# Relu pieces and rests of k taken off GpSimd, rests of q put on it, in a biased attention with two MLPs

## The chip, the core and the metric

The kernel runs on one NeuronCore of one Trainium2 chip. The metric is the device time of one execution in microseconds (us). In the profile's rows PE is TensorE, PEld its weight loads, DVE VectorE, ACT ScalarE, POOL GpSimd and SP SyncE, which issues nearly all transfers. L208 is line 208 of the kernel before.

## What is computed

The attention has 2 batches, 8 heads, 576 positions and a head size of 64. Each head gets a bias from a small network of the relative position; the result then runs through two MLPs (1152 tokens, width 512).

```python
scores = scale * np.matmul(q, k.transpose(0, 1, 3, 2))
psi_rel = np.log1p(np.abs(rel))
psi_i = np.log1p(np.maximum(pos[:, None].astype(np.float32), 1.0))
x = (psi_rel / psi_i)[..., None]
h = np.maximum(x @ w1 + b1, 0.0)
bias = h @ w2
scores = scores + bias.transpose(2, 0, 1)[None, :, :, :]
attn = np.exp(scores - max); attn = attn / (sum + 1e-09)
...
x = _moe_ref(...)       # (h * clip(h + 3, 0, 6) / 6) @ w_out, h = x @ w_in
x = _moe2_ref(...)      # (x @ w_a * (x @ w_b)) @ w_out
```

## The kernel before

The kernel is written engine by engine in a fixed order: each engine runs its instructions in the order of the code, and waits by semaphores where it needs another's result. It has three stages.

**The bias ahead of the attention (0 to 31.7 us).** The rows of the bias are made in 36 sets of 16 rows (`s`, later `g`). For one set, `bias_relu` makes four relu pieces `ht` of 128 partitions and `Dd` columns (576 for set 0, falling by 16 a set to 304 at set 17, then rising again to 576 at set 35): each is one instruction over the table `ltab`, on VectorE (L208), ScalarE (L210) or GpSimd (L212) by a letter in a string such as `"VVGA"`. `bias_parts` multiplies the four pieces by `w2` on TensorE (L227) and takes the result out of PSUM into a tile `E`, in forward order on ScalarE (L235) and reversed on VectorE (L244; in the attention steps mostly on ScalarE, L242), and then SyncE writes `E` to a scratch in DRAM (L256). The first ten sets (0 to 9) are done here. Sets 0 to 7 make up the first 128 rows of the bias, which SyncE then reads back (`bias_load`, L276). Even sets and the last two use `"VVVA"`, sets 1, 3, 5, 7 use `"VVGA"`; the pieces of GpSimd for these four lie in tiles of their own (`early`) and are issued ahead of the loop. All this has pools of two sets' buffers (`h`, 8 buffers) and four of `E`.

**The attention (31.7 to about 192 us)** in 36 steps `n`, each for 128 query rows and two heads. A step multiplies q by k (L307), where q and k are each split into a rounded part and a rest, so that the precision of f32 is kept: `q_hi`/`k_hi` round (ScalarE L141 and L167, VectorE L171, GpSimd L169), `q_lo`/`k_lo` subtract (L146, L175). `KS` holds the rounded k of two heads in partitions 0 to 63 and the rest in 64 to 127, and every L307 reads all 128 of them: a step needs both parts of its k. Then VectorE adds the bias and takes the minimum of the negated scores, in two instructions of 576 columns (L313, a custom one and a read of the accumulator each), ScalarE takes the exponential (L317, two of them), VectorE adds 1e-9 to the two sums (L321) and takes their reciprocals (L325), GpSimd scales P by them (L330, two instructions), and one step later TensorE transposes P (L340, L350), which VectorE (L341, L354) and ScalarE (L352) copy out of PSUM; another step later comes P times v (L365, L368), taken out by L377 (ScalarE) and L383 (VectorE). Steps 0 to 25 also carry one set of the bias each (sets 10 to 35), whose four pieces were made in the step before, by `"VVGA"`. `q_lo(n + 2)` is issued near the end of step `n`: on VectorE in steps 0 to 25, on GpSimd in the few left.

The order within a step on VectorE is: two L313, two L208, L321, L325, L383, L146, L341, L354, and then what the table `K_PLAN` has for the end of the step. Its entries are a step (-1 is ahead of step 0, 1.5 is within step 2), and what is done: a rounded part (`hi`), a rest (`lo`) or a load of k for the pair of heads `j`, on the engine given. Steps 0 to 7 are the first to use the pairs `j` = 0 to 7.

**The MLPs (192 to 619 us)** are matmuls on TensorE with the work around them on the other engines.

Of the kernel before, what the change touches and what calls it, by code (L numbers as in the profile page):

```python
# [21 lines left out]
NSET = S // 16  # L22
# [13 lines left out]


K_PLAN = {
    -1: (("hi", 2, "A"), ("lo", 2, "V"), ("hi", 3, "A"), ("hi", 4, "A"), ("lo", 3, "G"), ("load", 6, None)),
    1.5: (("lo", 4, "G"),),  # L40
    2: (("hi", 5, "V"),),
    3: (("lo", 5, "G"), ("load", 7, None), ("hi", 6, "A")),
    4: (("lo", 6, "V"),),
    5: (("hi", 7, "V"), ("lo", 7, "G")),
}
U32 = mybir.dt.uint32

# [2 lines left out]
def kernel(ctx, tc, cons, qm, qt, kt, vm, vt, wm, out):  # L50
# [31 lines left out]
    negb = ph.tile([128, 1], F32, name="negb")  # L82
    cst4 = ph.tile([128, 1], F32, name="cst4")
    cst3 = ph.tile([128, 1], F32, name="cst3")
    RELU = "VVGA"


    idle = ph.tile([128, S], F32, tag="h", bufs=8, name="idle")
# [84 lines left out]
    def k_lo(j, eng):  # L173
        hi, lo = (KS[64 * i : 64 * i + 64, 2 * j : 2 * j + 2, :] for i in range(2))
        eng.tensor_tensor(out=lo, in0=kr[j], in1=hi.bitcast(F32), op=ALU.subtract)  # L175
# [13 lines left out]
    extra = {}
    for i in range(2):  # L190
        t = pb.tile([128, 9, 128], F32, tag="PT", bufs=2, name="early").rearrange("p a n -> p (a n)")
        extra[1 + 4 * i], extra[3 + 4 * i] = t[:, 0:S], t[:, S : 2 * S]

    def bias_relu(s, kinds=RELU, only=None):

        i0, R, Dd = bias_geom(s)
        if s not in h_tiles:
            h_tiles[s] = [ph.tile([128, S], F32, tag="h", bufs=8, name="ht") for _ in range(4 if s not in extra else 3)]
            if s in extra:
                h_tiles[s].insert(kinds.index("G"), extra[s])  # L200
        for j in range(4):
            kind = kinds[j]
            if only is not None and kind not in only:
                continue
            ht = h_tiles[s][j]
            sc = scl[:, 4 * s + j : 4 * s + j + 1]
            if kind == "V":
                V.tensor_scalar(ht[:, :Dd], ltab[:, :Dd], scalar1=sc, scalar2=negb, op0=ALU.mult, op1=ALU.max)  # L208
            elif kind == "A":
                A.activation(ht[:, :Dd], ltab[:, :Dd], AF.Relu, bias=b1c, scale=sc)  # L210
            else:
                G.tensor_scalar(ht[:, :Dd], ltab[:, :Dd], scalar1=sc, scalar2=negb, op0=ALU.mult, op1=ALU.max)  # L212

    def bias_parts(s, rev, wide=False, kinds=RELU):

        i0, R, Dd = bias_geom(s)
        hs = h_tiles.pop(s)
        cst = cst3 if "A" in kinds else cst4
# [11 lines left out]
        def leave(c, bp, d0, d1):  # L230
            f1 = min(d1, S - i0)
            if f1 > d0 and not wide and n > 1 and c == 0:
                V.tensor_scalar(E[:, R + d0 : R + f1], bp[:, : f1 - d0], scalar1=8.0, scalar2=cst[:, 0:1], op0=ALU.mult, op1=ALU.add)
            elif f1 > d0:
                A.activation(E[:, R + d0 : R + f1], bp[:, : f1 - d0], AF.Identity, bias=cst[:, 0:1], scale=8.0)  # L235
            r0, r1 = max(d0, 1), min(d1, R + 1)
            if r1 > r0:
                src = bp[:, r0 - d0 : r1 - d0]
                dst = E[:, R - r1 + 1 : R - r0 + 1]
                dst = bass.AP(dst.tensor, dst.offset + (r1 - r0 - 1), [dst.ap[0], [-1, r1 - r0]])  # L240
                if rev is A and (wide or n == 1 or c):
                    A.activation(dst, src, AF.Identity, bias=cst[:, 0:1], scale=8.0)  # L242
                else:
                    V.tensor_scalar(dst, src, scalar1=8.0, scalar2=cst[:, 0:1], op0=ALU.mult, op1=ALU.add)  # L244

        if wide:
            for x in [mm(c) for c in range(n)]:
# [185 lines left out]
    for n in range(NSTEP):  # L433
# [3 lines left out]
        if n + 2 < 32:  # L437
            q_hi(n + 2)
        qk_units(n)
        k_work(n - 0.5)  # L440
        rest = bias_parts(g, A) if g < NSET else iter(())
        if g < NSET and bias_geom(g)[2] > 512:
            next(rest)
        if g + 1 < NSET:
            bias_relu(g + 1, only="V")
            bias_relu(g + 1, only="G")
        if n >= 2:
            pv(n - 2)
            x_hi(n - 2)
# [717 lines left out]
```

## Time and profile before

| what | value |
|---|---|
| median of 3 runs | 621.02 us (620.87 to 621.02) |
| the profiled execution | 620.63 us, of which the span of the trace is 618.9 us |
| mean granted clock of TensorE | 0.992 of 2.4 GHz |
| busy share of the span | PE 96%, DVE 74%, ACT 56%, POOL 47% |
| q1, the queue of nearly all transfers | 70.71 MB, 37.4% of 16 engines' span |

Busy shares are means over the three stages, so they are no measure of any one of them. The time of the profiled execution is 1.7 us more than its span, which runs from the first to the last instruction. Ends of matmuls are modelled in the records: a PE that is busy all the time need not be at its peak.

### The profile page before, as it was taken

The page shows a single profiled execution, that of the slowest core. Times are in us where ns is not written, and L with a number is a line of the kernel's source. Part 1 is how long each engine was busy: PE and PEld are TensorE (multiplying, and loading weights), DVE is VectorE, ACT ScalarE, POOL GpSimd, SP SyncE. Part 2 cuts the span into 40 slices and gives each one's busy share as a digit, 9 for nine tenths or more (in the row PEclk, how much of TensorE's full clock was granted, in tenths as well). Part 3 has the DMA queues.
Part 4 walks back from the last instruction along what each step waited for, and adds up shares of the span by engine and source line. Part 5 has one row for each costly group of instructions (what it writes and reads, how often), then busy time and mean ns, then how long its engine had stood idle before and what let it go on. Part 6 is the DMA issues. An engine that isn't in the chain of part 4 may idle for free. (4 is left out here: it accounts for less than half of the span.)

```text
span 618.9 us, 11234 instructions
## 1 busy us (share of the span) xinstructions
PE 595.3 (96%) x4234; PEld 526.8 (85%) x4234; DVE 460.5 (74%) x902; ACT 347.6 (56%) x718; POOL 293.0 (47%) x234
## 2 busy tenths in 40 slices
PE   8778899999999999999999999899999999999997
PEld 3265777777878999999999999889978999899986
DVE  7989999998666895697796565887495476956362
ACT  6777899987776664562462253455436454245310
POOL 7398878885764332221212143156334753368200
PEclk9979999999999999999999999999999999999999
DMA  8785745546933345244343220101235111510013
GB/s 259 221 262 157 233 129 185 175 131 198 274 83 104 103 127 179 70 135 144 104 128 105 66 68 35 35 1 34 69 108 164 38 67 38 169 67 1 1 53 101
DMA packets 28357, 71.50 MB, mean 116 GB/s; under 512 B 5392, under 2 KB 5776, under 8 KB 28304
## 3 DMA queue, kind: packets, MB, share of 16 engines
q1 hardware_dynamic: 28160, 70.71, 37.4%
q8 instruction: 33, 0.54, 0.4%
q14 instruction: 20, 0.16, 0.1%
q10 hardware_dynamic: 144, 0.09, 0.0%
HBM read 57.53 MB, written 13.25 MB: 114 GB/s over the span
## 5 line engine op out<-in xcount | busy, mean ns | idle before, releaser
L987 POOL TENSOR_TENSOR slot<-wv,slot 128x512 fp32r<-128x512 f32 x86 | 117.3, 1370 | 230.8 <-ACT slot L986 151.1
L541 PE MATMUL pair<-xx,slot 128*128 128x384 f32 x576 | 101.5, 335 | 0.0
L541 PEld LDWEIGHTS pair<-xx,slot 128*128 128x128 f32 x576 | 99.8, 188 | 0.1
L541 PE MATMUL pair<-gh,slot 128*128 128x384 f32 x384 | 98.6, 336 | 0.0
L747 PE MATMUL pair<-xx,slot 128*128 128x288 f32 x576 | 83.5, 296 | 2.5 <-DVE part L618 2.0
L747 PEld LDWEIGHTS pair<-xx,slot 128*128 128x128 f32 x576 | 78.6, 188 | 3.9 <-issue 2.3
L330 POOL TENSOR_SCALAR P<-P,st 128x576 f32<-128x576 f32 x72 | 61.0, 859 | 33.5 <-DVE st L325 18.5
L955 ACT ACTIVATE wv<-raw 128x512 f32<-128x512 f32 x63 | 42.4, 674 | 57.4 <-DMA raw<-in_wm_dram 32.7
L541 PEld LDWEIGHTS pair<-gh,slot 128*128 128x128 f32 x384 | 69.4, 188 | 0.1
L317 ACT ACTIVATE P<-P,st 128x576 f32<-128x576 f32 x72 | 55.4, 770 | 24.5 <-DVE st L313 24.3
L541 PE MATMUL pair<-slot,gh 128*128 128x512 f32 (+1 forms) x224 | 68.2, 387 | 0.6 <-ACT part L888 0.6
L747 PE MATMUL pair<-tt,slot 128*128 128x288 f32 x432 | 64.4, 298 | 1.4 <-ACT u L833 1.4
L541 PE MATMUL pair<-gl,slot 128*128 128x384 f32 x192 | 64.6, 336 | 0.9 <-DVE gl L559 0.9
L986 ACT CAST slot<-wv 128x512 fp32r<-128x512 f32 x86 | 53.1, 621 | 21.8 <-PE pair L747 12.8
L747 PEld LDWEIGHTS pair<-tt,slot 128*128 128x128 f32 x432 | 59.1, 188 | 3.3 <-ACT u L833 2.5
L313 DVE CUSTOM_DVE_ANT_0 P<-sc,bias 128x576 f32<-128x576 f32 x72 | 52.0, 754 | 7.0 <-PE sc L307 4.4
L566 ACT ACTIVATE t<-pair,three 128x384 f32<-128x384 f32 x48 | 27.9, 582 | 46.4 <-PE pair L541 46.3
L212 POOL TENSOR_SCALAR ht<-cs,scl,negb 128x416 f32<-128x416 f32 (+17 forms) x26 | 47.4, 1824 | 6.9 <-PE bpw L227 6.4
L208 DVE TENSOR_SCALAR ht<-cs,scl,negb 128x576 f32<-128x576 f32 (+17 forms) x78 | 50.0, 685 | 0.0
L541 PEld LDWEIGHTS pair<-slot,gh 128*128 128x128 f32 x224 | 41.3, 188 | 9.9 <-ACT part L888 1.0
L567 DVE SCALAR_TENSOR_TENSOR u<-t,pair 128x384 f32<-128x384 f32 x48 | 26.5, 551 | 27.2 <-ACT t L566 26.9
L964 DVE TENSOR_SCALAR wm<-wv 128x512 uint32<-128x512 uint32 x59 | 40.5, 687 | 4.5 <-ACT wv L955 4.3
(113 smaller groups left out, 1087.6 us busy)
## 6 DMA issues: line engine op xcount, KB each, us to landing
raw<-in_wm_dram SPq DMA_DIRECT2D x68, 512.0 KB, 3.5
scr<-E SPq DMA_DIRECT2D x36, 295.5 KB, 3.4
qraw<-in_qm_dram SPq DMA_DIRECT2D x8, 512.0 KB, 5.1
bias<-scr SPq DMA_DIRECT2D x7, 576.0 KB, 4.5
bias<-scr SPq DMA_DIRECT2D x7, 512.0 KB, 6.0
kraw<-in_kt_dram SPq DMA_DIRECT2D x8, 288.0 KB, 4.5
VM<-in_vm_dram SPq DMA_DIRECT2D x2, 1024.0 KB, 7.1
out_dram<-part SPq DMA_DIRECT2D x7, 256.0 KB, 2.0
```

The costliest lines, as they stand in the source:

```text
L208: V.tensor_scalar(ht[:, :Dd], ltab[:, :Dd], scalar1=sc, scalar2=negb, op0=ALU.mult, op1=ALU.max)
L212: G.tensor_scalar(ht[:, :Dd], ltab[:, :Dd], scalar1=sc, scalar2=negb, op0=ALU.mult, op1=ALU.max)
L313: V.tensor_tensor_reduce(out=Pu, in0=sc[:, :, 0:288], in1=bt, scale=-0.125, scalar=3.0e38, op0=ALU.add, op1=ALU.min, accum_out=st[:, u : u ...
L317: A.activation(P[:, u, :], P[:, u, :], AF.Exp, bias=st[:, u : u + 1], scale=-1.0, accum_out=st[:, 2 + u : 3 + u])
L330: G.tensor_scalar(P[:, u, :], P[:, u, :], scalar1=st[:, 2 + u : 3 + u], scalar2=1.0, op0=ALU.mult, op1=ALU.mult)
L541: T.matmul(ps_ap, l, r, start=(i == 0), stop=(i == len(prods) - 1))
L566: A.activation(t, hp, AF.Relu, bias=three[:, 0:1])
L747: T.matmul(pair[:, j, 0:TQ], l, r, start=start and i == 0, stop=i == 5, skip_group_check=not start)
L955: self.nc.scalar.mul(self.u[k], up, 2.0**-112)
L964: V.tensor_scalar(mid, ub, scalar1=3, scalar2=0x7FFFFFFF, op0=ALU.logical_shift_left, op1=ALU.bitwise_and)
L986: nc.scalar.copy(s[:, 0, :], v)
L987: nc.gpsimd.tensor_tensor(out=s[:, 1, :], in0=v, in1=s[:, 0, :].bitcast(F32), op=ALU.subtract)
```

## The change

GpSimd makes no relu pieces any more: every set uses three on VectorE and one on ScalarE, and the `early` tiles go. Of k, `k_hi(1)` goes from GpSimd to ScalarE and `k_lo(1)` from GpSimd to VectorE, one set later; `k_lo` 3, 4, 5 and 7 go from GpSimd to VectorE, at the ends of steps 0, 1, 3 and 6; `k_hi` 5 and 7 go from VectorE to ScalarE. `q_lo` of steps 0 to 25 goes from VectorE to GpSimd, behind its two L330.

```diff
 K_PLAN = {
-    -1: (("hi", 2, "A"), ("lo", 2, "V"), ("hi", 3, "A"), ("hi", 4, "A"), ("lo", 3, "G"), ("load", 6, None)),
-    1.5: (("lo", 4, "G"),),
-    2: (("hi", 5, "V"),),
-    3: (("lo", 5, "G"), ("load", 7, None), ("hi", 6, "A")),
+    -1: (("hi", 2, "A"), ("lo", 2, "V"), ("hi", 3, "A"), ("hi", 4, "A")),
+    0: (("lo", 3, "V"), ("load", 6, None)),
+    1: (("lo", 4, "V"),),
+    2: (("hi", 5, "A"),),
+    3: (("lo", 5, "V"), ("load", 7, None), ("hi", 6, "A")),
     4: (("lo", 6, "V"),),
-    5: (("hi", 7, "V"), ("lo", 7, "G")),
+    5: (("hi", 7, "A"),),
+    6: (("lo", 7, "V"),),
 }
...
-    RELU = "VVGA"
+    RELU = "VVVA"
...
-    mix = ("VVVA", "VVGA") * 4 + ("VVVA",) * LEAD
-    bias_relu(0, mix[0])
+    bias_relu(0)
     V.tensor_scalar(cst4, bps0[:, 0:1], scalar1=8.0, scalar2=None, op0=ALU.mult)
     V.tensor_copy(cst3[0:96], cst4[0:96])
-    for s in (1, 3, 5, 7):
-        bias_relu(s, mix[s], only="G")
     for s in range(8 + LEAD):
         if s < 7 + LEAD:
-            bias_relu(s + 1, mix[s + 1], only="VA")
-        bias_mm(s, V, wide=True, kinds=mix[s])
+            bias_relu(s + 1)
+        bias_mm(s, V, wide=True)
         if s in (1, 3):
             load_k(2 + s // 2)
         elif s == 5:
-            k_hi(1, G)
-            k_lo(1, G)
+            k_hi(1, A)
+        elif s == 6:
+            k_lo(1, V)
...
-        k_work(n - 0.5)
...
             bias_relu(g + 1, only="V")
-            bias_relu(g + 1, only="G")
...
-            q_lo(n + 2, V if g < NSET else G)
+            q_lo(n + 2, G)
```

On VectorE in the bias stage, sets 6 to 8 stand so before (an L208 row is the relu pieces of one set, L244 the reversed part of the set before it):

```order
L208 TENSOR_SCALAR ht<-cs,scl,negb 128x480 x3
L244 TENSOR_SCALAR E<-bpw,cst_83 128x95
L208 TENSOR_SCALAR ht<-cs,scl,negb 128x464 x2
L244 TENSOR_SCALAR E<-bpw,cst_83 128x111
L208 TENSOR_SCALAR ht<-cs,scl,negb 128x448 x3
L244 TENSOR_SCALAR E<-bpw,cst_83 128x127
```

and so in the change, where L202, L235 and L177 are the old L208, L244 and L175 (`KS<-kraw,KS` is a `k_lo`):

```order
L202 TENSOR_SCALAR ht<-cs,scl,negb 128x480 x3
L235 TENSOR_SCALAR E<-bpw,cst_83 128x95
L202 TENSOR_SCALAR ht<-cs,scl,negb 128x464 x3
L235 TENSOR_SCALAR E<-bpw,cst_83 128x111
L177 TENSOR_TENSOR KS<-kraw,KS 64x1152
L202 TENSOR_SCALAR ht<-cs,scl,negb 128x448 x3
L235 TENSOR_SCALAR E<-bpw,cst_83 128x127
```

The odd set has one more piece, and `k_lo(1)` stands ahead of the last relu that comes before the reversed part of set 7.

On VectorE, from the relu of step 1 to the start of step 2, there stands before (L146 is `q_lo`):

```order
L208 TENSOR_SCALAR ht<-cs,scl,negb 128x384 x2
L321 TENSOR_SCALAR st<-st 128x2
L325 RECIPROCAL st<-st 128x2
L146 TENSOR_TENSOR ql<-qraw,qh 128x256
L341 COPY PT<-sc 128x128
L354 COPY PT<-tp 128x512
L313 ISA P,st<-sc,bias 128x576
```

and in the change:

```order
L202 TENSOR_SCALAR ht<-cs,scl,negb 128x384 x3
L312 TENSOR_SCALAR st<-st 128x2
L316 RECIPROCAL st<-st 128x2
L332 COPY PT<-sc 128x128
L345 COPY PT<-tp 128x512
L177 TENSOR_TENSOR KS<-kraw,KS 64x1152
L304 ISA P,st<-sc,bias 128x576
```

One relu piece is added, `q_lo` is gone, and `k_lo(4)` stands between the last copy and the L313 of the next step (L304 in the change).

On GpSimd, steps 0 to 2 stand so before:

```order
L175 TENSOR_TENSOR KS<-kraw,KS 64x1152
L212 TENSOR_SCALAR ht<-cs,scl,negb 128x400
L330 TENSOR_SCALAR P<-P,st 128x576 x2
L212 TENSOR_SCALAR ht<-cs,scl,negb 128x384
L330 TENSOR_SCALAR P<-P,st 128x576 x2
L175 TENSOR_TENSOR KS<-kraw,KS 64x1152
L212 TENSOR_SCALAR ht<-cs,scl,negb 128x368
```

and every step of the change reads:

```order
L321 TENSOR_SCALAR P<-P,st 128x576 x2
L148 TENSOR_TENSOR ql<-qraw,qh 128x256
L321 TENSOR_SCALAR P<-P,st 128x576 x2
L148 TENSOR_TENSOR ql<-qraw,qh 128x256
L321 TENSOR_SCALAR P<-P,st 128x576 x2
```

Its step is now two scalings of P and one rest of q, and nothing runs on it ahead of step 0.

## Rows read from the trace of the kernel before

**Rows 1.** Windows: busy us (and instructions) of each engine, granted clock, DMA share, GB/s.

```profile
31.70:72.20 40.50, 33.56 (x290) 25.18 (x291) 37.93 (x96) 31.28 (x77) 35.33 (x28) 0.92 0.66 208
72.20:131.80 59.60, 59.60 (x604) 46.19 (x603) 57.74 (x169) 56.01 (x141) 48.83 (x43) 1.00 0.52 160
```

**Rows 2.** Timeline of PE, steps 13 and 14: start us, us, instruction.

```profile
95.22 0.33 PE L340 MATMUL sc<-ident,P 128*128 128x128 f32 x1
...
99.46 0.33 PE L340 MATMUL sc<-ident,P 128*128 128x128 f32 x1
```

**Rows 3.** Timeline of PE, steps 27 and 28, which carry no bias set.

```profile
156.54 0.33 PE L340 MATMUL tpb<-ident,P 128*128 128x128 f32 x1
...
159.99 0.33 PE L340 MATMUL tpb<-ident,P 128*128 128x128 f32 x1
```

**Rows 4.** Timeline of DVE: relu pieces of sets 0, 5, 6 and 15.

```profile
4.47 1.97 DVE L208 TENSOR_SCALAR ht<-cs,scl,negb 128x576 f32<-128x576 f32 x3
...
14.15 3.91 DVE L208 TENSOR_SCALAR ht<-cs,scl,negb 128x496 f32<-128x496 f32 x2
...
18.19 1.40 DVE L208 TENSOR_SCALAR ht<-cs,scl,negb 128x480 f32<-128x480 f32 x3
...
51.89 2.58 DVE L208 TENSOR_SCALAR ht<-cs,scl,negb 128x336 f32<-128x336 f32 x2
```

**Rows 5.** Timeline of POOL: two rests of k, scalings of P, a relu, a rest of q.

```profile
15.12 2.66 POOL L175 TENSOR_TENSOR KS<-kraw,KS 64x1152 fp32r<-64x1152 f32 x1
...
51.25 2.66 POOL L175 TENSOR_TENSOR KS<-kraw,KS 64x1152 fp32r<-64x1152 f32 x1
...
55.64 2.64 POOL L330 TENSOR_SCALAR P<-P,st 128x576 f32<-128x576 f32 x2
...
93.36 1.72 POOL L212 TENSOR_SCALAR ht<-cs,scl,negb 128x400 f32<-128x400 f32 x1
...
155.76 0.74 POOL L146 TENSOR_TENSOR ql<-qraw,qh 128x256 fp32r<-128x256 f32 x1
```

**Rows 6.** Timeline of ACT and DVE: set 5, three roundings of k, steps 3 and 4.

```profile
19.25 0.67 ACT L235 ACTIVATE E<-bpw,cst 128x496 f32<-128x496 f32 x1 [2.68 <-PE bpw L227]
...
27.05 3.25 ACT L167 CAST KS<-kraw 64x1152 fp32r<-64x1152 f32 x3
...
48.93 0.17 DVE L321 TENSOR_SCALAR st<-st 128x2 f32<-128x2 f32 x1 [0.27 <-ACT P L317]
...
52.14 0.79 ACT L317 ACTIVATE P<-P,st 128x576 f32<-128x576 f32 x1
```

**Rows 7.** Timeline of DVE and SP: from set 7 to the first L313.

```profile
22.97 0.35 DVE L244 TENSOR_SCALAR E<-bpw,cst 128x127 f32<-128x127 f32 x1
...
26.55 0.34 SPq L276 DMA_DIRECT2D bias<-scr  x1
...
31.72 0.76 DVE L313 CUSTOM_DVE_ANT_0 P<-sc,bias 128x576 f32<-128x576 f32 x1 [1.29 <-DMA bias<-scr]
```

**Rows 8.** Timeline of DVE: the rest of k behind step 4, the start of step 8.

```profile
56.36 1.39 DVE L175 TENSOR_TENSOR KS<-kraw,KS 64x1152 fp32r<-64x1152 f32 x1
...
72.19 0.75 DVE L313 CUSTOM_DVE_ANT_0 P<-sc,bias 128x576 f32<-128x576 f32 x1
```

**Rows 9.** Timeline of DVE, step 13.

```profile
92.87 0.76 DVE L313 CUSTOM_DVE_ANT_0 P<-sc,bias 128x576 f32<-128x576 f32 x1
...
94.23 1.07 DVE L208 TENSOR_SCALAR ht<-cs,scl,negb 128x400 f32<-128x400 f32 x2
95.33 0.17 DVE L321 TENSOR_SCALAR st<-st 128x2 f32<-128x2 f32 x1
...
95.81 0.42 DVE L146 TENSOR_TENSOR ql<-qraw,qh 128x256 fp32r<-128x256 f32 x1
...
97.09 0.76 DVE L313 CUSTOM_DVE_ANT_0 P<-sc,bias 128x576 f32<-128x576 f32 x1
```

**Rows 10.** Windows: steps 0 and 1, columns as in rows 1.

```profile
35.00:38.30 3.30, 2.57 (x13) 1.28 (x14) 3.27 (x11) 3.30 (x9) 3.19 (x3) 0.50 1.09 340
```

More of the change, by code (lines that the diff above doesn't have):

```diff
@@ L186, in bias_geom, with bias_relu @@
         return i0, R, max(R, S - 1 - i0) + 1
[L189 to L194, printed above, removed]
+    def bias_relu(s, only=None):
         i0, R, Dd = bias_geom(s)
         if s not in h_tiles:
-            h_tiles[s] = [ph.tile([128, S], F32, tag="h", bufs=8, name="ht") for _ in range(4 if s not in extra else 3)]
-            if s in extra:
-                h_tiles[s].insert(kinds.index("G"), extra[s])
+            h_tiles[s] = [ph.tile([128, S], F32, tag="h", bufs=8, name="ht") for _ in range(4)]
         for j in range(4):
-            kind = kinds[j]
+            kind = RELU[j]
             if only is not None and kind not in only:
@@ L208, in bias_relu, with bias_parts @@
                 V.tensor_scalar(ht[:, :Dd], ltab[:, :Dd], scalar1=sc, scalar2=negb, op0=ALU.mult, op1=ALU.max)
-            elif kind == "A":
+            else:
                 A.activation(ht[:, :Dd], ltab[:, :Dd], AF.Relu, bias=b1c, scale=sc)
-            else:
-                G.tensor_scalar(ht[:, :Dd], ltab[:, :Dd], scalar1=sc, scalar2=negb, op0=ALU.mult, op1=ALU.max)
-    def bias_parts(s, rev, wide=False, kinds=RELU):
+    def bias_parts(s, rev, wide=False):
         i0, R, Dd = bias_geom(s)
         hs = h_tiles.pop(s)
-        cst = cst3 if "A" in kinds else cst4
         n = 1 if Dd <= 512 else 2
@@ L232, in leave @@
             if f1 > d0 and not wide and n > 1 and c == 0:
-                V.tensor_scalar(E[:, R + d0 : R + f1], bp[:, : f1 - d0], scalar1=8.0, scalar2=cst[:, 0:1], op0=ALU.mult, op1=ALU.add)
+                V.tensor_scalar(E[:, R + d0 : R + f1], bp[:, : f1 - d0], scalar1=8.0, scalar2=cst3[:, 0:1], op0=ALU.mult, op1=ALU.add)
             elif f1 > d0:
-                A.activation(E[:, R + d0 : R + f1], bp[:, : f1 - d0], AF.Identity, bias=cst[:, 0:1], scale=8.0)
+                A.activation(E[:, R + d0 : R + f1], bp[:, : f1 - d0], AF.Identity, bias=cst3[:, 0:1], scale=8.0)
             r0, r1 = max(d0, 1), min(d1, R + 1)
@@ L241, in leave @@
                 if rev is A and (wide or n == 1 or c):
-                    A.activation(dst, src, AF.Identity, bias=cst[:, 0:1], scale=8.0)
+                    A.activation(dst, src, AF.Identity, bias=cst3[:, 0:1], scale=8.0)
                 else:
-                    V.tensor_scalar(dst, src, scalar1=8.0, scalar2=cst[:, 0:1], op0=ALU.mult, op1=ALU.add)
+                    V.tensor_scalar(dst, src, scalar1=8.0, scalar2=cst3[:, 0:1], op0=ALU.mult, op1=ALU.add)
         if wide:
```

## The prediction

> **What bounds the kernel now.** I read the windows of the stages first. In steps 8 to 21 (72.2 to 131.8 us) TensorE, VectorE and ScalarE are all busy for 94% or more, at the full clock; in steps 0 to 7 VectorE is busy for 37.9 of 40.5 us and TensorE for only 33.6 [rows 1]. The reader is tempted to call VectorE the bound of both. So I went to TensorE's timeline for the wait that a busy share can't show. From the first transpose of step 13 to that of step 14 it is 4.24 us, and nothing stands idle between [rows 2]; in steps 27 and 28, where no bias set is made and VectorE waits, the same stretch takes 3.45 us [rows 3]. The difference, 0.79, is what a bias set's eight matmul rows take in step 13. TensorE's pieces have the same distances in both, so I take it that TensorE sets the pace in steps 8 to 21. There the change can give nothing, only take.
>
> What is left is the bias stage and steps 0 to 7. In the first, VectorE is the engine that the others wait for. While GpSimd runs a rest of k (15.12 to 17.78), VectorE's two relu pieces of set 5 take 3.91 us [rows 4, 5]; three pieces of set 6, with GpSimd idle, take 1.40 [rows 4]. ScalarE then waits 2.68 us for TensorE, which waits for that relu [rows 6]. The end of the stage is a chain: the reversed part of set 7 on VectorE at 22.97, its write, the read of the bias issued at 26.55, and the first L313 at 31.72, which waited 1.29 us for that transfer [rows 7].
>
> In steps 0 to 7 the picture repeats: in step 4 the relu pieces of set 15 take 2.58 us beside GpSimd's rest of k at 51.25 [rows 4, 5], and a rest of k on VectorE itself lies open between the last copy and the next L313, 1.39 us [rows 8].
>
> **The bias stage, part by part.** From 4.47 us, where VectorE's relu begins, to the reversed part of set 7 it is 18.5 us [rows 4, 7]. Undisturbed, one piece costs 0.44 us from start to start at 480 columns, (1.40 - 0.52) / 2 [rows 4]. The change has 27 pieces there, nine sets of three, of 512 columns on average; I take 0.455 each, between 0.44 and 0.47 (in proportion): 12.3 us, bounds 11.9 and 12.7. The seven reversed parts and two constants stay (some 1.6 us). `k_lo(1)` is new on VectorE: 1.4 [rows 8]. That is 15.3 us. To it come waits for ScalarE, whose forward part a reversed part follows. `E` starts about 1.2 us after the last relu of its set (set 5: 19.25, after 14.15 + 3.91 [rows 4, 6]) and takes 0.67; counted through, this leaves VectorE waiting 0.45 us at set 4, and 0.8 at set 6, since `k_hi(1)` now stands ahead of that set on ScalarE, (3.25 - 1.15) / 2 = 1.05 us [rows 6]. In all 16.5, and so 2.0 us less than now. What follows, the write, the wait and the read, I take over unchanged at 8.75 us [rows 7]: what VectorE has to do meanwhile (three more pieces, three rests, a rounding) ends 1 us before the bias lands. So the first L313 comes at 29.7 instead of 31.72. Bounds: 0, if the transfers and not their issue set when the bias lands, and 3.0, if no wait for ScalarE is left.
>
> **Steps 0 to 7.** Four durations carry the sum. The two L313 take 1.36 us and are followed by the relu [rows 9], now three pieces of 0.35 to 0.40. From L321 to the next L313 it is 1.76 us [rows 9], of which `q_lo` is 0.33 (its 0.42 less what overlaps the next): 1.43 is left. A rest of k in this gap adds 1.40 [rows 8]. And ScalarE needs 3.21 us from L321 to its next L317 if a rounding of k stands between [rows 6], so 2.16 without; L321 follows L317 by 1.66 (two exponentials of 0.77 each and the read of a sum), or the third relu, whichever is later. From the first L313:
>
> Step 0: relu done at 2.8, `k_lo(3)`, next L313 at 4.5. Step 1: `k_lo(3)` holds GpSimd's scaling of P, as in step 4 now, where two scalings take 2.64 instead of some 1.6 [rows 5]; so `q_lo(2)` runs until 6.5 and holds the first relu by 0.65; L321 at 7.45, `k_lo(4)`, L313 at 10.05. Step 2 is free: L321 at 12.6, L313 at 14.0. Step 3: `k_hi(5)` puts L317 at 15.8 and L321 at 17.45, `k_lo(5)` puts L313 at 20.3. Step 4: `k_hi(6)` is hidden beside `k_lo(5)`; L321 at 22.75, `k_lo(6)`, L313 at 25.6. Step 5: 29.5. Step 6: `k_hi(7)` puts L321 at 32.9; L354 ends at 34.35, and `k_lo(7)` runs till 35.75. Here is a wait that is new: step 7 reads pair 7, and its L307 now stands behind `k_lo(7)`, with all of TensorE behind it: 0.85 us from there to L313, at 36.6. Step 8, TensorE's pace again: 40.7. Now it is 72.19 - 31.72 = 40.47 [rows 7, 8]. So the sum over these steps is +0.25: what GpSimd's rests no longer hold is paid back by VectorE's own. Bounds: -1.5, if half of the delays of steps 1 and 6 don't come, and +2.0, if roundings and rests never hide beside one another.
>
> How long `q_lo` holds a relu in step 1 is a choice between rows. GpSimd's own relu of step 13 runs from 93.36 to 95.08, and VectorE's two pieces beside it, from 94.23, take 1.07 us against about 0.9 undisturbed [rows 5, 9]: one of them is held, by some 0.2. A rest of k on GpSimd holds the piece for all its time (51.25 to 53.91, two pieces 51.89 to 54.47 [rows 4, 5]). `q_lo` is a subtraction of the same kind, so I take the full 0.65; by the relu's row it would be 0.2, and the sum 0.45 lower. The Trainium skill (SBUF — State Buffer, Who interferes with whom) says that GpSimd shares one pair of ports with a VectorE instruction in a two-port mode, and that whichever starts first holds it for its whole instruction: by that it is 0.65 and the sum stays. The trace agrees for the rests of k, not for GpSimd's relu.
>
> **Steps 8 to 25 and after.** VectorE's chain in a step of 400 columns becomes 1.36 + 1.2 + 1.43 = 4.0 us, against TensorE's 4.24. `q_lo` on GpSimd takes 0.74 [rows 5] behind two scalings of about 0.8, so it ends some 2.85 us after L321 and 0.25 before the next relu. I cost both at nothing; they lie beside TensorE. If the gap were gone, `q_lo` would hold a relu by up to 0.74, and a step would grow by that less VectorE's slack of 0.24. From step 26 on the instructions are the same as now; I put nothing there.
>
> **The sum.** -2.0 + 0.25 = -1.75 us against the profiled execution's 620.63, so 618.9. The median of the runs is 0.39 above that execution: 619.3. For this kernel a measurement tells a change from none at about 0.2%, 1.24 us, so that faster means below 619.8 and slower above 622.3.
>
> **Rivals.** *VectorE paces steps 8 to 25 after all.* Then each gets 0.24 us shorter, 18 of them 4.3 us: 615.0. The 94% of ScalarE and VectorE speak for it, the equal distances of TensorE's pieces [rows 2, 3] against. 0.10.
>
> *The transfers end the bias stage.* The DMA share is near 1 while the first bias is read; 1.09 a little later [rows 10]. If the bytes ahead of that read set its landing, the 2.0 us turn into a longer wait of L313 and the rest is +0.25: 621.3, no change. Against: that read is issued behind the write of set 7, which VectorE's reversed part at 22.97 lets go [rows 7]. 0.21.
>
> *TensorE's clock stays low longer.* Around step 1 the granted clock is 0.50, the 1.2 GHz level [rows 10]; a mean of 0.92 over steps 0 to 7 says that this lasts some 6.5 of 40.5 us [rows 1]. The change makes step 0 longer by 1 us on VectorE, with TensorE idle. If step 2 then lies at the low level as a whole, TensorE needs 8.4 us for it, not 4.0: 4.4 more, 623.7. It decides from 3.0 us more. For it speaks the longer idle time, against it that a stay as long as now ends within step 2, and that step 3 waits for ScalarE in any case. 0.10.
>
> *GpSimd gives back what it takes.* If `q_lo` meets the relu in full in every step of 8 to 25, it costs 0.5 us in each, 9 us: 628. It decides from an overlap of 0.4 us a step. The 0.25 us between them speak against it. 0.04. The Trainium skill (Perfetto Trace Analysis, Optimizing Scalar/DVE Operations) warns of this, since the two share a read port; the trace has no `q_lo` of GpSimd beside a relu, so it neither agrees nor differs here.
>
> **How the numbers follow.** The forecast has 0.55, from 618.0 to 620.4 by itself; of that 0.43 lies below 619.8. With the first rival that is 0.53 for faster. No change has 0.36: 0.12 of the forecast, 0.21 of the transfers, 0.03 of a short stay of the clock. Slower has 0.11. The range that leaves out 2 in 10 reaches from 617.0, towards the first rival, to 621.9, past the transfers' case.
>
> **What would show it.** Right: set 7's reversed part at about 21.0 and the read of the bias at about 24.5; the first L313 at 29.7; step 8's L313 40.7 us behind it; step 13 at 4.24, as now. L307 of step 7 waiting for the rest of pair 7, and L321 of steps 3 and 6 waiting for ScalarE. Wrong: relu pieces longer than 0.5 us in steps 8 to 25, a first L313 with a wait for transfers above 3 us, a granted clock of 0.5 past step 2, or steps of 4.0 us.

## The result, and the profile after

The change made the kernel slower: 624.53 us (median of 5 runs, 623.46 to 625.35) against 620.87 us before (619.95 to 621.02, runs beside it). The ratio is 1.0056, with a 95% interval from 1.0040 to 1.0073, so 3.5 us more (2.5 to 4.5). The forecast was 619.3, with a range from 617.0 to 621.9. The profiled execution took 623.59 us, 2.96 more than that of before, and its span is 621.8. Line numbers have moved: L313 is now L304, L307 L298, L317 L308, L321 L312, L330 L321, L340 L331, L350 L341, L368 L359, L208 L202, L244 L235, L146 L148, L175 L177, L276 L267, L953 L940.

Where the 2.9 us of the span went is read from the starts of the steps, each the first L313 (L304) on VectorE:

| stretch | before | after | difference | forecast |
|---|---|---|---|---|
| up to the first L313 | 31.72 | 30.14 | -1.58 | -2.0 |
| steps 0 to 7 | 40.47 | 43.82 | +3.35 | +0.25 |
| steps 8 to 28 | 89.67 | 89.64 | -0.03 | 0 |
| step 29 | 4.41 | 5.53 | +1.12 | 0 |
| step 30 to the end | 452.6 | 452.7 | 0 | 0 |

These are two single executions. A second profile of each kernel (below) has 32.45 and 29.86 in the first row, 39.98 and 44.08 in the second, 4.71 and 5.06 in the fourth: the same signs, other sizes.

The windows of the changed kernel, steps 0 to 2 together, steps 3, 4, 5, 6 and 7 one by one, then steps 8 to 21 (columns as in [rows 1]; the granted clock is the value behind the five engines):

```profile
30.14:44.08 13.94, 11.31 (x77) 8.24 (x76) 13.57 (x35) 10.15 (x25) 7.33 (x8) 0.72 0.82 284
44.08:50.97 6.89, 6.34 (x68) 4.70 (x70) 5.73 (x14) 6.89 (x15) 4.13 (x6) 1.00 0.78 246
50.97:56.71 5.74, 4.54 (x47) 3.32 (x43) 5.64 (x13) 3.96 (x11) 3.27 (x4) 1.00 0.41 110
56.71:60.44 3.73, 2.69 (x24) 1.96 (x17) 3.69 (x13) 2.93 (x8) 1.27 (x2) 1.00 0.17 55
60.44:68.33 7.89, 4.38 (x45) 3.29 (x44) 5.65 (x15) 5.80 (x14) 4.73 (x6) 1.00 0.58 174
68.33:73.96 5.63, 5.63 (x45) 4.16 (x45) 4.01 (x12) 4.12 (x10) 2.17 (x3) 0.70 0.48 166
...
73.96:133.71 59.75, 59.73 (x605) 46.25 (x604) 55.16 (x170) 55.46 (x139) 29.38 (x41) 1.00 0.52 159
```

Two rows stand out. In step 6 every engine is idle for over 2 of 7.89 us, and in step 7 TensorE is busy all the time at a mean clock of 0.70. The last row answers to the second of [rows 1]: VectorE has 2.6 us less to do there and GpSimd 19 less, and yet nothing is shorter, since TensorE is busy for all of it.

What happened between steps 6 and 7 is on TensorE's timeline of the changed kernel, with one row of VectorE's:

```profile
63.79 0.27 PE L341 MATMUL tp<-ident,P 128*128 128x128 f32 x1
67.41 0.51 PE L298 MATMUL sc<-KS,qh 128*128 128x288 f32 x2 [3.34 <-DVE KS L177]
...
69.06 1.98 PE L359 MATMUL pvb<-PT,VM 128*64 128x128 f32 x16
...
68.33 0.76 DVE L304 CUSTOM_DVE_ANT_0 P<-sc,bias 128x576 f32<-128x576 f32 x1 [1.07 <-PE sc L298]
```

and in its window of the low clock:

```profile
68.56:71.97 3.41, 3.41 (x28) 2.06 (x26) 2.86 (x10) 2.43 (x6) 0.61 (x1) 0.50 0.72 256
```

TensorE stands idle for 3.34 us until VectorE's rest of pair 7 (L177) is done, and VectorE then waits 1.07 us for TensorE. The idle stretch ends at 67.41, and from 68.56 to 71.97 the granted clock is 0.50, the 1.2 GHz level: the sixteen L359 (P times v) take 1.98 us, and in step 6 they took 1.09.

The rests of k on VectorE (L177) beside GpSimd's work, its scalings of P (L321) and its rest of q (L148), in step 3 (first three rows) and at the end of step 0 (last two), from the timelines of both engines:

```profile
48.99 0.74 POOL L321 TENSOR_SCALAR P<-P,st 128x576 f32<-128x576 f32 x1
49.08 1.86 DVE L177 TENSOR_TENSOR KS<-kraw,KS 64x1152 fp32r<-64x1152 f32 x1
49.71 1.83 POOL L148 TENSOR_TENSOR ql<-qraw,qh 128x256 fp32r<-128x256 f32 x1
...
33.31 1.35 DVE L177 TENSOR_TENSOR KS<-kraw,KS 64x1152 fp32r<-64x1152 f32 x1
33.46 2.55 POOL L321 TENSOR_SCALAR P<-P,st 128x576 f32<-128x576 f32 x2 [32.11 <-ACT ht L204]
```

In step 3 GpSimd's second scaling began 0.09 us before the rest of k, and the rest takes 1.86, 0.51 more than its 1.35; it is the same in steps 4 and 6. In step 0 the rest began first: it takes 1.35, and the two scalings take 2.55 instead of 1.47.

The head of the attention, and step 29, on the timelines of VectorE, GpSimd and TensorE:

```profile
22.12 0.34 DVE L235 TENSOR_SCALAR E<-bpw,cst 128x127 f32<-128x127 f32 x1
...
28.69 1.35 DVE L177 TENSOR_TENSOR KS<-kraw,KS 64x1152 fp32r<-64x1152 f32 x1
30.14 0.76 DVE L304 CUSTOM_DVE_ANT_0 P<-sc,bias 128x576 f32<-128x576 f32 x1
...
166.72 0.65 POOL L940 TENSOR_SCALAR wv<-raw 128x512 f32<-128x512 f32 x1 [1.36 <-DMA raw<-in_wm_dram]
...
168.45 0.46 PE L356 MATMUL pvb<-PT,VT 128*128 128x128 f32 x2 [1.03 <-DVE xx L374]
```

The first L304 follows the rest of pair 2 after 0.10 us; the wait of 1.29 us for the bias that [rows 7] show is gone. In step 29 GpSimd waits 1.36 us for the first weights of the MLPs, then VectorE for GpSimd, and TensorE 1.03 us for VectorE. The row of before that answers to it:

```profile
163.87 0.68 POOL L953 TENSOR_SCALAR wv<-raw 128x512 f32<-128x512 f32 x1 [0.25 <-DMA raw<-in_wm_dram]
```

### The profile page after: what moved, and what is told of

It is laid out like the page before. It is cut to its first block, busy times and chain, and to the rows that moved or that the text cites. A ratio compares the mean times of both kernels' runs of the same rounds, so it can differ in the third digit from the quotient of the medians.

```text
span 621.8 us, 11226 instructions
## 1 busy us (share of the span) xinstructions
PE 596.8 (96%) x4234; PEld 529.0 (85%) x4234; DVE 456.0 (73%) x909; ACT 350.5 (56%) x721; POOL 239.2 (38%) x224
## 5 line engine op out<-in xcount | busy, mean ns | idle before, releaser
L321 POOL TENSOR_SCALAR P<-P,st 128x576 f32<-128x576 f32 x72 | 57.5, 812 | 103.3 <-DVE xx L374 39.4
L308 ACT ACTIVATE P<-P,st 128x576 f32<-128x576 f32 x72 | 55.4, 770 | 26.4 <-DVE st L304 26.2
L304 DVE CUSTOM_DVE_ANT_0 P<-sc,bias 128x576 f32<-128x576 f32 x72 | 52.1, 755 | 6.9 <-PE sc L298 5.0
L202 DVE TENSOR_SCALAR ht<-cs,scl,negb 128x576 f32<-128x576 f32 (+17 forms) x108 | 48.7, 507 | 0.1
L957 DVE SCALAR_TENSOR_TENSOR wv<-raw,wm 128x512 uint32<-128x512 uint32 x59 | 40.5, 686 | 3.9
```

The lines of the kernel that those rows point to most:

```text
L304: V.tensor_tensor_reduce(out=Pu, in0=sc[:, :, 0:288], in1=bt, scale=-0.125, scalar=3.0e38, op0=ALU.add, op1=ALU.min, accum_out=st[:, u : u ...
L308: A.activation(P[:, u, :], P[:, u, :], AF.Exp, bias=st[:, u : u + 1], scale=-1.0, accum_out=st[:, 2 + u : 3 + u])
L321: G.tensor_scalar(P[:, u, :], P[:, u, :], scalar1=st[:, 2 + u : 3 + u], scalar2=1.0, op0=ALU.mult, op1=ALU.mult)
L957: V.scalar_tensor_tensor(out=v, in0=self.words(k, 0), scalar=29, in1=mid, op0=ALU.logical_shift_right, op1=ALU.bitwise_or)
```

## The experiments

Four theories were on the table. **A**: the bias stage gains what its row shows, and the change loses in steps 0 to 7, by VectorE's rests of k, which collide with GpSimd, and by the one for which TensorE stands idle and then runs at a low clock. **B**: an earlier start of the attention is worth nothing, since transfers come at their own time. **C**: VectorE's work is simply longer in these steps, and a rest of k costs the same wherever it stands. **D**: step 29 waits for weights that are issued too late. Ratios are to the kernel before, run beside each on the same chip; a ratio of 0.001 is 0.62 us.

### The bias stage alone

```diff
-    mix = ("VVVA", "VVGA") * 4 + ("VVVA",) * LEAD
-    bias_relu(0, mix[0])
+    bias_relu(0, "VVVA")
...
         elif s == 5:
-            k_hi(1, G)
-            k_lo(1, G)
+            k_hi(1, A)
+        elif s == 6:
+            k_lo(1, V)
```

> The kernel before with the bias stage of the change alone: all ten sets there with three relu pieces on VectorE, the rounding of pair 1 on ScalarE and its rest on VectorE; K_PLAN, the relu by VVGA in the steps and the rest of q on VectorE stay as before. Theory A (the change gains 1.6 us in the bias stage and loses some 3.4 us in steps 0 to 7, each for itself): first L313 at 30.1 us instead of 31.72, and the gain lasts: about 1.6 us less than before, 619.3. Rival B (an earlier start of the attention meets transfers that land no earlier, so that the gain would be lost whatever the steps hold): first L313 at 30.1, but step 8 at 72.2 as before, or the gain lost by step 30: 620.9.

Measured: ratio 0.9972 (0.9959 to 0.9985), 1.7 us less. Theory A holds for this stage and B falls: the gain lasts to the end. VectorE's timeline of this run:

```profile
21.09 0.34 DVE L237 TENSOR_SCALAR E<-bpw,cst 128x127 f32<-128x127 f32 x1
...
29.40 0.76 DVE L306 CUSTOM_DVE_ANT_0 P<-sc,bias 128x576 f32<-128x576 f32 x1 [0.80 <-DMA bias<-scr]
```

Here VectorE makes only two relu pieces of set 10, is done earlier, and the transfer of the bias ends the stage again, at 29.40. In its step 7 the clock was at 0.50 for 3.4 us too, behind a step 6 in which TensorE was idle for 1.7 us in two pieces (more on this under the weights below); its runs lie between 618.4 and 621.6.

### The clock behind the wait: two fillers

```diff
         k_work(n)
+        if n == 6:
+            for _ in range(28):
+                T.transpose(sc_tiles[n][:, 1, 288:416], ident, ident)
```

> The changed kernel with 28 more transposes of the identity on TensorE, behind the transposes of step 6 and ahead of the products q times k of step 7, into columns of PSUM that nobody reads: about 3.1 us of work in the 3.34 us for which TensorE waits for the rest of pair 7. Nothing waits less. Theory A (TensorE's idle stretch of 3.34 us is what brings the clock down to 0.50 from 68.56 to 71.97): granted clock 1.0 in step 7, which takes 4.05 us instead of 5.63; the time is 1.6 us less than that of the change, 622.9. Rival: the low stretch has another cause, the clock falls all the same, and the time stays at 624.5.

Measured: 1.0065 (1.0046 to 1.0085), no gain, though the clock of step 7 did what theory A says: step 7 at 1.00 and 4.06 us long. In the profiled execution the filler ended late and held the products by 0.4 us, so that step 6 took 8.33, and steps 29 and 30 took 10.3 us together, since the first two weights kept GpSimd waiting for 2.03 and 1.41 us; in the change they take 8.84. It also had 3.4 us at 0.50 near 404 us, in the MLPs, where the first profile of the change has none. So the time did not tell what the filler is worth, and it was tried again with 22 transposes, beside weights that are loaded early (that edit stands below, under the weights that step 29 waits for).

> The changed kernel with the early weights of the earlier run and 22 transposes of the identity as a filler in step 6 (28 ended 0.4 us behind the rest of pair 7 and held the products of step 7; 22 should end just ahead of it). With early weights alone steps 6 and 7 took 8.41 + 6.22 us, with 6.8 us of granted clock at 0.50 from 66.83 on. Theory A (TensorE's idle stretch brings the clock down): clock 1.0 in step 7, steps 6 and 7 take 7.9 + 4.07 us, 2.6 us less than with early weights alone: a ratio of about 0.999 to before. Rival (the filler run's time, no less than the change's, is the true one: the clock that is gained in step 7 is lost elsewhere): 1.003 as with early weights alone.

Measured: 0.9984 (0.9974 to 0.9995), against 1.0032 (1.0019 to 1.0046) for early weights alone. A is borne out: work that nobody needs, put into TensorE's idle time, makes the kernel with early weights 3.0 us faster. TensorE's timeline of this run:

```profile
64.12 2.62 PE L483 MATMUL sc<-ident 128*128 128x128 f32 x22 [0.77 <-DVE PT L332]
66.69 0.51 PE L298 MATMUL sc<-KS,qh 128*128 128x288 f32 x2
...
68.14 1.09 PE L359 MATMUL pvb<-PT,VM 128*64 128x128 f32 x16
```

and its windows of steps 6 and 7:

```profile
59.73:67.62 7.89, 6.96 (x67) 5.68 (x66) 5.66 (x15) 5.80 (x14) 4.73 (x6) 1.00 0.56 169
67.62:71.67 4.05, 4.05 (x45) 3.27 (x45) 3.80 (x12) 3.25 (x9) 1.02 (x2) 1.00 0.70 241
```

Step 6 is as long as in the change, 7.89 us; step 7 is not 5.63 but 4.05, and the L359 take 1.09 us again. In the run with early weights alone the two steps took 14.64 us, here 11.94.

### The rest of pair 7 in the middle of its step

The added call asks the table for `n + 0.5`, so that 6.5 lies within step 6.

```diff
-    6: (("lo", 7, "V"),),
+    6.5: (("lo", 7, "V"),),
...
+        k_work(n + 0.5)
         denominators(n)
         reciprocals(n)
```

> The changed kernel with the rest of pair 7 on VectorE in the middle of step 6, behind its relu pieces and ahead of L312, instead of at its end. VectorE waits 1.10 us there for the exponential, and GpSimd has no rest of q to make at that time. Theory A: the rest takes 1.35 to 1.4 us, not 1.85, and ends at 64.3, not 67.3; L312 comes 0.3 later, the next L304 at 65.7; step 6 takes 5.25 us instead of 7.89, and with TensorE idle for less than 1 us at a time the clock stays at 1.0 and step 7 takes 4.05, not 5.63. In all 4.2 us less than the change: 620.3. Rival C (VectorE's work is simply longer in these steps, and a rest costs the same wherever it stands): only the wait of 1.07 us goes, 623.4.

Measured: 0.9956 (0.9941 to 0.9971). Moving one instruction of 1.35 us makes the changed kernel some 6 us faster, 2.7 us below before. VectorE's timeline of this run:

```profile
63.52 1.35 DVE L177 TENSOR_TENSOR KS<-kraw,KS 64x1152 fp32r<-64x1152 f32 x1
...
66.17 0.74 DVE L304 CUSTOM_DVE_ANT_0 P<-sc,bias 128x576 f32<-128x576 f32 x1
```

and its windows of steps 6 and 7:

```profile
61.01:66.17 5.16, 4.60 (x45) 3.35 (x44) 5.06 (x15) 5.16 (x13) 2.17 (x4) 1.00 0.36 72
66.17:70.19 4.02, 4.02 (x45) 3.24 (x44) 3.79 (x14) 3.88 (x11) 2.48 (x5) 1.00 0.98 336
```

C falls: the rest lies where VectorE waited for the exponential, takes 1.35 us, and L304 follows the last copy without a wait. Between the two profiled executions it is 4.4 us (623.59 to 619.15), as theory A had it. The ratios give more; why is not shown, but the change's steps 6 and 7 are not always as short as in its first profile (14.9 and 14.6 us in the two other runs that have them with little else changed).

### What slows a rest of k: q's rest, or the scalings of P

```diff
-            q_lo(n + 2, G)
+            q_lo(n + 2, V if n in (3, 4, 6) else G)
```

> The changed kernel with the rest of q on VectorE instead of GpSimd in steps 3, 4 and 6, the three in which VectorE's rest of k takes 1.86 us. Theory A (the two subtractions, each with two inputs in SBUF, slow one another): L177 takes 1.35 to 1.4 us in these steps, and each is 0.47 - 0.33 = 0.14 us shorter: about 0.4 less in all. Rival (the rest of k is slow there for another reason, transfers or TensorE's reads among them): L177 still takes 1.86, and the three steps grow by 0.33 each, 1.0 in all.

Measured: one execution, 624.67 us (the kernel before beside it has a median of 621.72). This form of theory A falls: with no rest of q on GpSimd, L177 still takes 1.71 us, and steps 3 and 4 are 0.2 us longer, at 7.08 and 5.92. But the causes that the rival names (transfers, TensorE's reads) aren't needed either, as the timelines of the two engines show:

```profile
48.05 0.74 POOL L321 TENSOR_SCALAR P<-P,st 128x576 f32<-128x576 f32 x1
48.28 1.71 DVE L177 TENSOR_TENSOR KS<-kraw,KS 64x1152 fp32r<-64x1152 f32 x1
```

The rest of k began 0.23 us behind the scaling, where in the change it was 0.09, and is held 0.36 us instead of 0.51. What fits both is that it is held by the scaling that was there first and then runs its 1.35 us whatever comes. GpSimd's `q_lo`, which comes last, is the one that waits: in the change it takes 1.83 us and ends 0.6 behind the rest of k.

So all rests of pairs 4 to 7 were put where GpSimd has nothing to do:

```diff
-    1: (("lo", 4, "V"),),
+    1.5: (("lo", 4, "V"),),
...
-    3: (("lo", 5, "V"), ("load", 7, None), ("hi", 6, "A")),
-    4: (("lo", 6, "V"),),
+    3.5: (("lo", 5, "V"), ("load", 7, None)),
+    3: (("hi", 6, "A"),),
+    4.5: (("lo", 6, "V"),),
...
-    6: (("lo", 7, "V"),),
+    6.5: (("lo", 7, "V"),),
```

> The changed kernel with four rests of k on VectorE (of pairs 4, 5, 6 and 7) in the middle of steps 1, 3, 4 and 6, behind the relu pieces and ahead of L312, instead of at the ends. Theory A in the form that the runs so far leave of it: VectorE's rest of k is held by a scaling of P that GpSimd began before it (L321 at 48.99, the rest at 49.08, 1.86 us, of which 1.35 its own), and waits for the exponential stand open in steps 3 and 6. In the middle of a step GpSimd has nothing to do, so all four rests take 1.35 to 1.40 us; step 3 takes about 5.3 us instead of 6.90, step 4 5.25 instead of 5.74, step 6 5.2 instead of 7.89, step 7 4.05 instead of 5.63: from the first L304 to that of step 8 37.3 us, not 43.82. Some 2 us less than with the rest of pair 7 alone in the middle. Rival C (VectorE's work is simply longer, and a rest costs the same wherever it stands; or the later scalings of P hold TensorE's transposes): steps 3 and 4 stay at 6.9 and 5.7, and the time at that of the run with pair 7 alone.

Measured: 0.9962 (0.9946 to 0.9977). The steps came as expected, the time did not: every L177 (L178 here) takes 1.35 us, step 3 takes 5.25 and step 4 5.22 us; the time is no better than with pair 7 alone. In the profiled run step 2 took 6.15 us, not 3.8, with the clock at 0.50 from 33.67 to 43.91. That is what the third rival of the forecast had for step 2, in a kernel for which it was not put forward. Its runs lie between 617.0 and 620.6, so this may come and go; what decides it is not settled.

### The weights that step 29 waits for

```diff
+                ph.release()
+                pw0 = tc.alloc_tile_pool(name="pw0", bufs=1, side="left", reuse_waits="tile")
+                ring.add(pw0, 3, 4, 5)
+                ring.load()
+                ring.load()
+                ring.load()
                 bias_load(g // 8, 0)
...
-        if n == NSTEP - 9:
```

(The block under the last line went with it.)

> The changed kernel with the first three loads of MLP weights issued in step 25, ahead of the reads of the last bias, instead of in step 27 behind them. Theory D (step 29 takes 5.53 us and not 4.41 since the first weights land 7.2 us behind their issue, and GpSimd, VectorE and TensorE wait for one another behind them): the first L940 waits for no transfer, TensorE has no idle time in step 29, which takes 4.1 to 4.4 us; 1.1 us less than the change. Rival: the reads of the bias are late instead, and step 32 or 33 waits as long; no gain.

Measured: 1.0032 (1.0019 to 1.0046), 1.5 us less than the change. Theory D holds: step 29 takes 4.28 us, and no later step takes longer for it (step 32 4.68, step 33 4.56, as in the change). The same edit of the kernel before:

> The kernel before with the first weights issued ahead of the last bias, as in the run with the change. In its two profiles step 29 took 4.41 and 4.71 us. If the 1.1 us in step 29 belong to the change, this gives the kernel before only 0.2 to 0.4 us (ratio 0.9995); if late weights come and go in either kernel alike, it gains about as much as the change did by it, 0.24% (ratio 0.9976).

Measured: 0.9997 (0.9986 to 1.0008), no gain; step 29 takes 4.29 us. But its profile shows something else. Its step 7 takes 5.58 us and not 4.05, at the low clock. TensorE's timeline of steps 6 and 7 in the kernel before (first two rows) and in this run:

```profile
67.68 0.53 PE L307 MATMUL sc<-KS,qh 128*128 128x288 f32 x2 [0.97 <-DVE PT L341]
...
68.62 1.09 PE L368 MATMUL pvb<-PT,VM 128*64 128x128 f32 x16
...
66.95 0.78 PE L307 MATMUL sc<-KS,qh 128*128 128x288 f32 x2 [0.97 <-DVE PT L341]
...
68.57 1.98 PE L368 MATMUL pvb<-PT,VM 128*64 128x128 f32 x16
```

Step 6 has the same two idle pieces of TensorE, of 0.7 and 1.0 us, in both profiles of the kernel before, in this run and in that of the bias stage alone; in the first two step 7 ran at 1.00 (4.05 and 4.06 us), in the other two at 0.50 for 3.4 us (5.58 and 5.57). So the clock can fall in step 7 without the long wait of the change, in some executions. With that wait left as it is (3.3 to 3.5 us of idle TensorE) it fell in all four profiles (the change twice, the early weights, the rest of q on VectorE), and with the filler or the rest of pair 7 in the middle in none of five.

And the kernel before, unchanged:

> The kernel before, unchanged, for a second profile. If step 29 takes 4.4 us again, its 1.1 us more in the change belong to the change (it reaches that step in another state of the transfers); if it takes 5 us or more, that length comes and goes from run to run, and the 1.1 us are no effect of the change. The same is asked of the stretches of the granted clock at 0.50: before they were 10.2 us, with the change 13.7.

Measured: one execution, 621.17 us; step 29 takes 4.71 us, and the first weights are waited for 0.56 us. The clock was at 0.50 for 13.7 us in all, as in the change, not 10.2 as in the other profile of before, so that this sum is no mark of either kernel. In every profile with the bias stage of the change and without early weights, step 29 takes 5.06 us (the change a second time) to 5.87 (the first filler). So the longer wait goes with the change, and with its bias stage alone too (5.23). Why is open: from issue to use the first weights took 6.1 and 6.4 us in the two profiles of before and 7.2 in the change, while the same transfers stand ahead of them.

### The plan of before, and the change a second time

```diff
-    0: (("lo", 3, "V"), ("load", 6, None)),
-    1: (("lo", 4, "V"),),
...
+    1.5: (("lo", 4, "G"),),
+    2: (("hi", 5, "V"),),
+    3: (("lo", 5, "G"), ("load", 7, None), ("hi", 6, "A")),
     4: (("lo", 6, "V"),),
...
+    5: (("hi", 7, "V"), ("lo", 7, "G")),
```

(The entry -1 has the rest of pair 3 on GpSimd and load 6 again, and the call of the kernel before that makes 1.5 a place within step 2 is back.)

> The changed kernel with K_PLAN as before: rests 3, 4, 5 and 7 on GpSimd, k_hi 5 and 7 on VectorE; the third relu piece on VectorE and the rest of q on GpSimd stay as changed. Theory A (what the change loses lies in the rests of k at VectorE's step ends, and in what TensorE waits and loses of its clock behind the last of them): most of the loss is gone, step 7 starts without a wait for pair 7, and the time is near that of the bias stage alone, ratio 0.997 to 0.999. Rival: the third relu piece on VectorE and the rest of q on GpSimd, which in this kernel meets rests of k of 2.66 us on the same engine, cost as much; ratio 1.003 or more.

Measured: 1.0020 (1.0004 to 1.0035), between the two: neither theory A's 0.997 to 0.999 nor the rival's 1.003. With the plan of before the changed kernel is 2.2 us faster. VectorE starts step 7 without a wait (it takes 4.01 us), but TensorE waits 1.50 us for GpSimd's rest of pair 7 in step 6. And the rest of the plan is not free: timelines of this run at the head of the attention and in step 4,

```profile
28.39 2.62 POOL L175 TENSOR_TENSOR KS<-kraw,KS 64x1152 fp32r<-64x1152 f32 x1 [27.05 <-ACT KS L167]
28.54 3.69 DVE L175 TENSOR_TENSOR KS<-kraw,KS 64x1152 fp32r<-64x1152 f32 x1
32.26 0.76 DVE L302 CUSTOM_DVE_ANT_0 P<-sc,bias 128x576 f32<-128x576 f32 x1
...
51.48 3.51 DVE L200 TENSOR_SCALAR ht<-cs,scl,negb 128x336 f32<-128x336 f32 x3
51.67 2.76 POOL L175 TENSOR_TENSOR KS<-kraw,KS 64x1152 fp32r<-64x1152 f32 x1
```

show GpSimd's rest of pair 3, begun 0.15 us ahead of VectorE's of pair 2, hold it to 3.69 us, which throws the gain of the bias stage away (first L302 at 32.26), and a rest hold three relu pieces to 3.51 us, where [rows 4] had two in 2.58. This mixture meets collisions that neither kernel has, so it doesn't part the loss cleanly.

> The changed kernel itself for a second profile. By theory A steps 6 and 7 together take 13.5 to 14.9 us, as in the profile of the change (13.52) and in the two runs that leave these steps alone (14.92, 14.63), with the granted clock at 0.50 for one or two stretches behind the wait of step 6; step 29 takes over 5 us.

Measured: one execution, 623.59 us; steps 6 and 7 take 7.88 + 5.59 us, step 29 5.06. The clock is at 0.50 from 68.74 to 72.16, behind the same wait of 3.34 us.

### Both edits together

The rests of pairs 4 to 7 in the middle of their steps and the early weights, by the two diffs above.

> Both of the two edits before: rests of k in the middle of steps 1, 3, 4 and 6, and the first weights ahead of the last bias. If each saves what its theory says, some 7.5 us less than the change and 4 us less than before, about 617; if step 29's wait is one of transfers that come at their own time, the earlier arrival at step 29 only makes it longer in the first of the two, and this one gains 1 to 2 us on it.

Measured: 616.29 us, ratio 0.9925 (0.9907 to 0.9942): 4.7 us less than before and the fastest of all. Its windows of steps 0 to 2 and of steps 3 to 7 one by one:

```profile
29.53:43.71 14.18, 10.92 (x75) 7.84 (x76) 13.58 (x34) 10.54 (x26) 6.54 (x8) 0.76 0.80 277
43.71:48.96 5.25, 4.50 (x45) 3.38 (x45) 5.15 (x14) 5.25 (x13) 1.74 (x3) 1.00 0.79 242
48.96:54.18 5.22, 4.42 (x45) 3.33 (x44) 5.12 (x15) 5.12 (x12) 2.17 (x4) 1.00 0.56 180
54.18:58.26 4.08, 4.08 (x45) 3.24 (x44) 3.80 (x13) 3.29 (x9) 2.53 (x5) 1.00 0.29 78
58.26:63.44 5.18, 4.60 (x45) 3.41 (x45) 5.08 (x15) 5.18 (x13) 1.82 (x3) 1.00 0.38 90
63.44:67.46 4.02, 4.02 (x45) 3.24 (x44) 3.79 (x13) 3.50 (x10) 2.47 (x5) 1.00 1.03 348
```

Steps 3 to 7 take 23.75 us, in the change 29.88 and before 25.70. Instructions and engines are those of the change; only places differ. So the third relu piece on VectorE and the rest of q on GpSimd are not by themselves what the change loses by. Its step 29 takes 4.31 us, 1.1 less than with the rests alone; the ratios differ by more (2.3 us), and the low clock of step 2 was not in this profile.

## Why the prediction was wrong, point by point

- **TensorE sets the pace in steps 8 to 25: right.** The first transposes of steps 13 and 14 are 4.25 us apart, 4.24 before [rows 2], and steps 8 to 28 changed by 0.03 us in all. On TensorE's timeline of the changed kernel:

```profile
97.01 0.33 PE L331 MATMUL sc<-ident,P 128*128 128x128 f32 x1
...
101.26 0.33 PE L331 MATMUL sc<-ident,P 128*128 128x128 f32 x1
```

  With no step of 4.0 us the first rival did not come, and the fourth did not either: GpSimd's `q_lo` held no relu there (three pieces in 1.28 us at 400 columns).
- **The bias stage: right in mechanism, the size a little off.** The reversed part of set 7 was forecast at 21.0 and came at 22.12 in the first profile and at 21.14 in the second (why they differ is not shown); the first L304 was forecast at 29.7 and came at 30.14 and 29.86. "What VectorE has to do meanwhile ends 1 us before the bias lands" was wrong: VectorE's work behind that part ends 7.9 us after it (22.12 to 30.04), near the forecast's 7.75, but the bias lands sooner than the 8.75 that were taken over, within 8.0 us here and 8.3 in the first experiment, so that VectorE ends the stage. The transfers' rival fell with the first experiment. The kernel before is no fixed mark either: in its second profile the first L313 came at 32.45 and waited for TensorE.
- **"The sum over these steps is +0.25": this is the step that failed.** It measured +3.35, beyond its own bound of +2.0. Steps 0 to 2 are right (13.94 us; 14.0 forecast). Two terms are mis-sized behind them. First, a rest of k was put at 1.40 us wherever it stood. The row that it came from had the rest at 56.36 [rows 8]. GpSimd's relu and its second scaling in the same profile, and GpSimd's scalings in step 3 of the change (last row):

```profile
54.02 1.64 POOL L212 TENSOR_SCALAR ht<-cs,scl,negb 128x336 f32<-128x336 f32 x1
...
56.37 1.92 POOL L330 TENSOR_SCALAR P<-P,st 128x576 f32<-128x576 f32 x1
...
48.27 1.47 POOL L321 TENSOR_SCALAR P<-P,st 128x576 f32<-128x576 f32 x2 [2.76 <-DVE xx L374]
```

  The rest and the second scaling began within 0.01 us of each other, and the scaling paid. GpSimd had come to its scalings late there, at 55.64, since its relu ran until 55.66. In the change it has no relu, waits 2.76 us for VectorE and starts its scalings at 48.27, right behind the reciprocals (47.90); its second one comes 0.09 ahead of the rest, and the rest takes 1.86, 0.46 more than the 1.40, in each of steps 3, 4 and 6: 1.4 us. (That `q_lo` is gone from VectorE isn't the reason: with it back there, the scaling led by 0.23.) The forecast had both durations in its rows and did not ask which of the two began first. The Trainium skill (SBUF — State Buffer, Who interferes with whom) says just this: issue order, not the kind of operation, decides who blocks, and a VectorE instruction with two inputs in SBUF contends with a GpSimd instruction that reads SBUF. The rows of steps 0 and 3 and those of before agree, with 1.35, 1.86 and 1.39 us for one instruction.
- **The wait behind `k_lo(7)`: foreseen, and under-priced.** L304 of step 7 waited 1.07 us (0.85 forecast). The second mis-sized term is the clock, which was put at nothing here. TensorE's idle time is not VectorE's wait: it was 3.34 us, and behind it the clock was at 0.50 for 3.4 us, so that step 7 took 5.63 us and not 4.1. The filler shows it: without the idle stretch, with the same wait for pair 7, step 7 took 4.05. The third rival had the mechanism, and a time (623.7) near the result, at the wrong place: step 2. It was priced for the idle time of step 0, of 1 us more, and not asked of the longest new wait of the change. That neither profile of the kernel before has the low clock in step 7 is in part luck: two runs with its steps have it.
- **"From step 26 on the instructions are the same": true, and not enough.** Step 29 took 1.12 us more: the first weights, which came 0.25 us late before, came 1.36 us late. Between the second profiles it was 0.35. The experiments show that the wait is one for the weights, and that the change has more of it; they don't show why.
- **The holding of the relu in step 1 by `q_lo(2)`** was put at 0.65 us; three pieces took 1.64 us at 36.06 and 1.25 undisturbed at the same 384 columns (91.83), so it was 0.4.

So the sum, term by term, is -1.6 for the bias stage, the +0.25 of the forecast for steps 0 to 7, +1.4 for rests that come second, +0.2 and +1.5 for the wait and the clock behind it, and +1.1 for step 29: +2.85, against 2.9 between the spans of the two profiled executions. Since the terms are read from these two, that they add up says only that no stretch was left out. The medians are 0.7 us further apart than these executions, and which term holds that is not shown.

## What to carry to other kernels

Where a change makes two engines' instructions overlap that slow one another, a duration of the old profile holds for the old order of their starts alone: look which of the two began first, and by how much. The price of a wait is not the bottleneck's wait: follow it to TensorE, see how long that stands idle, and look in more than one trace what the clock did behind it. And put an instruction that waits for nobody into a wait of its own engine at a time when its rival is idle: four moved rests of k and three earlier loads, with no work taken away, turned +3.5 us into -4.7.

## What the runs showed of the hardware that was not expected

- One VectorE subtraction of 64x1152 takes 1.35 us alone, 1.71 and 1.86 when a GpSimd scaling began 0.23 and 0.09 us before it, and 3.69 behind a GpSimd subtraction of the same shape that began 0.15 us before. The one that began first kept nearly its own duration (0.74, 2.62). At a margin of 0.01 us the records don't tell the order: at 56.36 (before) and at 38.87 (step 1 of the change, the scaling at 38.86) it was the scaling that paid, with 1.92 and 1.93 us.
- 22 transposes without use, 2.6 us of work, made the kernel with early weights 3.0 us faster; 28, which ended 0.4 us late, gave no gain in the changed kernel.
- The granted clock falls at different places in executions of one kernel: for the kernel before from 28.1 to 31.6 and from 35.0 to 41.8 us in one profile, and from 18.4 to 21.8 as well in the other. The second profile of the change has 3.4 us at 0.50 from 403.3 on, in the MLPs, where its first has none; several of the experiments have such a stretch there, and others not. Such a stretch cost 1.5 us in step 7 (5.57 against 4.05), and one near 400 us some 0.6 (from step 30 to the end it is 452.6 to 452.7 us in the six profiles without it and 453.2 or more in the eight with it), so a difference of 1 to 2 us between two single executions of this kernel can be no more than that.
